# Batch 0 of a chunked attention with an MLP: transposes into one-bank PSUM tiles, values ahead of the last scores, zero matmuls moved, last copy on VectorE

## Chip, cores, metric

One core of a Trainium2 chip. The three later sets of runs were on three chips (8, 4 and 12 in the record: the runs a1 to a4, b1 to b4, c1 to c4), each with runs of the kernel before beside them. The metric is the device time of one execution in microseconds; the kernel before takes 233.71 us (median of the first three runs). PE is TensorE, ACT is ScalarE, DVE is VectorE, POOL is GpSimd.

Times of one kernel scatter here by about 2 us, more than the effect studied. So three things stand beside each time: the mean granted clock of the run (the share of TensorE's full clock that was let through), the start of the MLP in the trace, and the stretch from v2 to the MLP explained below.

## The reference, cut to what matters

```python
# q, k, v: (4 batches, 8 heads, 768, 64); 8 memory rows; windows of 32 queries
for c in range(768 // 32):
    k_full = concat([mem_k, k[:, :, c*32-16 : c*32+40]])     # v likewise
    scores = 0.125 * q_c @ k_full.T
    a = softmax(scores)
    out[:, :, c*32:c*32+32] = a @ v_full
x = out.transpose(0, 2, 1, 3).reshape(3072, 512)
h = x @ w_in                                                 # 512 -> 2048
s = sin(alpha * h)
y = (h + s * s / alpha) @ w_out                              # 2048 -> 512
```

## The kernel before, where it matters

The kernel works batch by batch. Batch 0's attention runs alone, ahead of batch 0's MLP, because nothing else has been loaded (in the first profile the loads of w_in are issued from 17.1 us on and land 6.5 to 12.9 us later). It is split into eight units, two for each pair of heads. A string gives the order in which their steps enter the engines' queues, each of which runs in order (in the first profile x2 starts at 20.69 us and v3, behind it in PE's queue, at 20.87): k and q are transposes of inputs, s scores, e exponentials, v values, x the transposes of a unit's result and their copy, and z a matmul on zeros. The tiles that this kernel's matmuls write are taken from two pools in PSUM: the smaller, [P, 512] in F32, are called one-bank tiles here, those of twice that size two-bank tiles.

```python
ORDER = (
    "k 0,q 0,memk 0,memv 0,k 1,s 0,e 0,z 1,s 1,e 1,q 1,k 2,s 2,e 2,s 3,v 0,q 2,e 3,k 3,x 0,v 1,q 3,s 4,e 4,x 1,"
    "s 5,e 5,v 2,z 1,s 6,e 6,x 2,v 3,z 1,s 7,e 7,x 3,z 1,v 4,z 1,v 5,x 4,z 1,v 6,x 5,z 1,v 7,x 6,z 1,x 7"
)
big = ...tile_pool(name="big", bufs=3, space=PSUM)   # tiles of two banks
smp = ...tile_pool(name="smp", bufs=2, space=PSUM)   # tiles of one bank

def spin(n, z=None):                       # z: n matmuls on zeros
    if z is None:
        z = smp.tile([P, 512], F32, name="z", tag="sm")
    for _ in range(n):
        nc.tensor.matmul(z[:], zeros[:, 0:P], zeros[:])

def pv(b, cells, pt):                      # v: values, then normalise on DVE
    ot = big.tile([P, 2, 512], F32, name="ot", tag="big")
    ...                                    # 8 matmuls into ot
    nc.vector.reciprocal(rv, otv[0:QW, :, :, D])
    nc.vector.tensor_tensor(out=x_blk..., in0=otv..., in1=rv..., op=ALU.mult)
    return x_blk, ot

def xt(dst, x_blk, ot, copy=nc.vector.tensor_copy):     # x: transpose, copy
    xtp = ot[:].bitcast(BF)[:, 0, 640:640 + KT * QW].rearrange("p (k c) -> p k c", k=KT)
    for kt in range(KT):
        nc.tensor.transpose(xtp[:, kt, :], x_blk[...], ident[0:QW, 0:QW])
    copy(dst, xtp)
...
# in the loop over ORDER
elif what == "e":
    ptl[n] = exps(cells[n], scl.pop(n))
    if n == 7:
        nc.scalar.activation(rows[:, 0:1], zeros[:, 0:1], ACTF.Sin)   # loads the sine table
elif what == "v":
    xbl[n] = pv(0, cells[n], ptl.pop(n))
elif what == "x":
    xt(xT[...], *xbl.pop(n), nc.vector.tensor_copy if n < 4 else nc.scalar.copy)
...
load_v(0, 0, 16)      # early; later, behind more of q and k:
load_v(0, 16, 32)     # values of units 2 and 3
load_v(0, 32, 64)     # values of units 4 to 7
```

The softmax here doesn't subtract the row's maximum and nothing guards it: scores larger than these inputs give would overflow.

## Time and profile before

| | kernel before, first profile |
|---|---|
| span in the trace | 232.2 us (the time adds about 1.8 us) |
| mean granted clock | 0.993 |
| first matmul of v2 | 19.27 us |
| first MLP matmul | 27.73 us |
| **v2 to MLP** | **8.46 us** |

"v2 to MLP" runs from the first value matmul of unit 2 to the first MLP matmul.

From the page of the kernel before, the slices of PE and of its clock (each digit is a tenth of a 5.8 us slice):

```profile
PE   7897899989999999999999999998999999899994
...
PEclk9998999999999999999999999999999999999999
```

PE is near full from slice 5 on, so an earlier MLP start should reach the end. The one dip of the clock, the 8 in the fourth slice, is half clock (0.50) over 3.4 us, from about 20.91 to 24.33 (read in windows of 0.1 us).

### The profile page before, as it was taken

What the parts mean: (1) busy time and instruction counts of PE and PEld (TensorE: products, weight loads), DVE (VectorE), ACT (ScalarE), POOL (GpSimd) and SP (SyncE); (2) the same over time, 40 slices, a digit from 0 to 9 for tenths busy, and PEclk for the clock granted to TensorE, in tenths of its full rate; (3) what the DMA queues carried; (4) which work ended last, traced back from release to release, by engine and by line L of the source; (5) the groups of instructions that cost most, each with busy time, mean ns of one, the idle gap of its engine ahead of it and who ended that gap; (6) DMA issues with size and microseconds to landing.
All of it is one profiled execution on the core that took longest, in us unless ns stands there. A gap on an engine that the chain in (4) does not pass through costs nothing.

```text
span 232.2 us, 4583 instructions
## 1 busy us (share of the span) xinstructions
PE 219.2 (94%) x1834; PEld 122.7 (53%) x1834; DVE 160.1 (69%) x287; ACT 153.0 (66%) x247; POOL 70.0 (30%) x80
## 2 busy tenths in 40 slices
PE   7897899989999999999999999998999999899994
PEld 3454565555446565654555656564555555453453
DVE  5775679888667897988467798887565458774110
ACT  3478689884887387898564877878664676880110
POOL 8999112595912115157300315020000020110000
PEclk9998999999999999999999999999999999999999
DMA  6999999999999910109992101010111010101112
GB/s 84 145 176 175 207 204 206 208 133 100 143 235 173 80 45 0 45 7 178 172 159 71 45 0 48 0 45 3 45 48 58 33 49 0 45 1 48 70 66 90
DMA packets 51805, 21.13 MB, mean 91 GB/s; under 512 B 36296, under 2 KB 48840, under 8 KB 51784
## 3 DMA queue, kind: packets, MB, share of 16 engines
q0 software_dynamic: 45568, 14.41, 68.7%
q1 hardware_dynamic: 6216, 6.43, 9.1%
q8 instruction: 14, 0.23, 0.4%
q14 instruction: 7, 0.06, 0.1%
HBM read 28.94 MB, written 6.29 MB: 152 GB/s over the span
## 4 chain that ended last, share of the span: by engine, by line
PE 64%; ACT 12%; DVE 11%; issue 5%; POOL 3%; DMA 2%; POOLq 1%; DVEq 0%; ACTq 0%
PE o L472 28%; PE hT L393 21%; DVE gT L422 5%; ACT u L405 4%; PE ot L301 3%; ACT pt L286 3%; PE sc L270 3%; DVE x_blk L306 2%; PE ot L316 2%; DMA k_bf<-in_k_dram 2%; DVE s L414 2%; ACT s L408 2%; PE tt_a L242 2%; PE o L461 2%; PE o L442 1%
## 5 line engine op out<-in xcount | busy, mean ns | idle before, releaser
L472 PE MATMUL o<-w_out_sb,gT 128*128 128x512 bf16 x336 | 90.0, 380 | 0.4 <-DVE gT L422 0.4
L393 PE MATMUL hT<-xT,w_in_sb 128*128 128x384 bf16 x488 | 87.1, 326 | 2.9 <-DVE gT L422 2.8
L422 DVE SCALAR_TENSOR_TENSOR gT<-s,inv_alpha,hT 128x768 bf16<-128x768 f32 x61 | 61.0, 1012 | 19.7 <-ACT s L408 11.6
L405 ACT ACTIVATE u<-hT,alpha_sb 128x768 f32<-128x768 f32 x61 | 54.7, 897 | 24.0 <-PE hT L393 22.9
L393 PEld LDWEIGHTS <-w_in_sb 128*128 128x128 bf16 x512 | 49.3, 98 | 37.5 <-issue 3.8
L286 ACT ACTIVATE pt<-sc,biasm 128x256 bf16<-128x256 f32 (+2 forms) x104 | 39.1, 470 | 15.1 <-PE sc L270 15.1
L472 PEld LDWEIGHTS <-gT 128*128 128x128 bf16 x336 | 29.3, 98 | 24.3 <-DVE gT L422 1.2
L410 POOL TENSOR_TENSOR s<-u 128x768 f32<-128x768 f32 x9 | 13.2, 1465 | 88.4 <-ACT u L405 61.3
L408 ACT ACTIVATE s<-u 128x768 f32<-128x768 f32 x32 | 27.0, 844 | 1.0
L414 DVE TENSOR_TENSOR s<-u 128x768 f32<-128x768 f32 x23 | 24.3, 1056 | 3.1 <-ACT u L405 3.0
L306 DVE TENSOR_TENSOR x_blk<-ot,rinv 96x512 bf16<-96x512 f32 x32 | 22.0, 687 | 1.1
L139 POOL DMA_DIRECT2D vw<-in_v_dram x24 | 22.0, 933 | 0.0
L216 POOL COPY pr<-q_bf 128x768 bf16<-128x768 bf16 x12 | 10.7, 894 | 35.4 <-PE tt_a L242 24.4
L430 DVE COPY o_sb<-o 128x512 f32<-128x512 f32 x12 | 8.3, 689 | 15.6 <-PE o L472 15.4
L430 ACT COPY o_sb<-o 128x512 f32<-128x512 f32 x11 | 6.4, 583 | 17.9 <-PE o L472 17.9
L305 DVE RECIPROCAL rinv<-ot 96x8 f32<-96x8 f32 x32 | 6.4, 201 | 15.8 <-PE ot L301 15.5
L301 PEld LDWEIGHTS <-pt 128*128 128x128 bf16 x256 | 12.4, 100 | 6.7 <-issue 2.2
L301 PE MATMUL ot<-vw,pt 128*128 128x65 bf16 x256 | 13.6, 197 | 0.9 <-ACT pt L286 0.9
L270 PEld LDWEIGHTS <-kTi 64*128 64x128 bf16 x256 | 6.9, 95 | 12.0 <-issue 5.9
L242 PEld LDWEIGHTS <-pr 128*128 128x128 bf16 x144 | 10.0, 98 | 5.9 <-DVE pr L216 0.9
L316 PE MATMUL ot<-ident,x_blk 96*128 96x96 bf16 x128 | 11.0, 208 | 2.1 <-DVE x_blk L306 2.0
L316 PEld LDWEIGHTS <-x_blk 96*128 96x128 bf16 x128 | 8.3, 98 | 8.4 <-DVE x_blk L306 3.8
(74 smaller groups left out, 171.1 us busy)
## 6 DMA issues: line engine op xcount, KB each, us to landing
out_dram<-o_sb SPq DMA_DIRECT2D x23, 256.0 KB, 2.0
k_bf<-in_k_dram POOLq DMA_DIRECT2D x3, 768.0 KB, 7.7
q_bf<-in_q_dram POOLq DMA_DIRECT2D x3, 768.0 KB, 12.4
vw<-in_v_dram POOLq DMA_DIRECT2D x6, 384.0 KB, 13.9
w_in_sb<-in_moe_w_in_dram POOLq DMA_DIRECT2D x4, 512.0 KB, 10.2
w_out_sb<-in_moe_w_out_dram POOLq DMA_DIRECT2D x2, 1024.0 KB, 24.8
k_bf<-in_k_dram POOLq DMA_DIRECT2D x4, 192.0 KB, 5.4
q_bf<-in_q_dram POOLq DMA_DIRECT2D x4, 192.0 KB, 5.4
```

The costliest lines, as they stand in the source:

```text
L139: nc.gpsimd.dma_start(dst, src)
L286: nc.scalar.activation(pt[:, 0:H * QW].rearrange("p (g e c) -> p e g c", g=4, e=2)[:, :, c0:c1, 32 * m:32 * m + 32], sc[:, :, 0:4 * QW].re ...
L301: nc.tensor.matmul(otv[:, n // 4, n % 4, :], pt[:, QW * n:QW * n + P], vws[b % 2][:, 2 * hp + n % 2, j, 0:D + 1])
L306: nc.vector.tensor_tensor(out=x_blk[:].rearrange("p (g e) d -> p g e d", g=2), in0=otv[0:QW, :, :, 0:D], in1=rv.unsqueeze(3).to_broadcast( ...
L316: nc.tensor.transpose(xtp[:, kt, :], x_blk[:, 2 * kt:2 * kt + 2, :].rearrange("p e d -> p (e d)"), ident[0:QW, 0:QW])
L393: nc.tensor.matmul(hts[hf][:, 0:HALF], w_in_sb[:, kt, P * ft:P * ft + P], xT[:, kt, HALF * hf:HALF * hf + HALF], start=(kt == 0), stop=(kt ...
L405: nc.scalar.activation(u[:], hT[:, :, 0:HALF], ACTF.Sin, scale=alpha_sb[:, ft:ft + 1])
L408: nc.scalar.activation(s2[:], u[:], ACTF.Square)
L414: nc.vector.tensor_tensor(out=s2[:], in0=u[:], in1=u[:], op=ALU.mult)
L422: nc.vector.scalar_tensor_tensor(out=gv, in0=s2[:], scalar=inv_alpha[:, ft:ft + 1], in1=hT[:, :, 0:HALF], op0=ALU.mult, op1=ALU.add)
L430: (nc.vector.tensor_copy if s % 2 == 0 else nc.scalar.copy)(o_sb[:], o[:])
L472: nc.tensor.matmul(o[:], gT[:, ft, P * s:P * s + P], w_out_sb[:, ft, :], start=(ft == 0), stop=(ft == FT - 1),)
```

## The change

The intent: PE should not stand behind a transpose that waits for DVE while a ready value product is queued behind it. So each v goes ahead of the previous x. To allow that, from unit 2 on x no longer uses v's tile, which is then free after the multiply. The values of unit 4 go ahead of the last scores. Zero matmuls move to where PE used to wait, with two ahead of each of the transposes. Copy 7 goes to DVE.

```diff
-    "s 5,e 5,v 2,z 1,s 6,e 6,x 2,v 3,z 1,s 7,e 7,x 3,z 1,v 4,z 1,v 5,x 4,z 1,v 6,x 5,z 1,v 7,x 6,z 1,x 7"
+    "s 5,e 5,z 1,v 2,s 6,e 6,z 2,v 3,x 2,v 4,s 7,e 7,x 3,v 5,x 4,v 6,x 5,v 7,x 6,x 7"
...
-        xtp = ot[:].bitcast(BF)[:, 0, 640:640 + KT * QW].rearrange("p (k c) -> p k c", k=KT)
+        if ot is None:
+            z = smp.tile([P, 512], F32, name="z", tag="sm")
+            spin(2, z)
+            xtp = z[:].bitcast(BF)[:, 0:KT * QW]
+        else:
+            xtp = ot[:].bitcast(BF)[:, 0, 640:640 + KT * QW]
+        xtp = xtp.rearrange("p (k c) -> p k c", k=KT)
...
-                xbl[n] = pv(0, cells[n], ptl.pop(n))
+                x_blk, ot = pv(0, cells[n], ptl.pop(n))
+                xbl[n] = x_blk, (ot if n < 2 else None)
...
-                   *xbl.pop(n), nc.vector.tensor_copy if n < 4 else nc.scalar.copy)
+                   *xbl.pop(n), nc.scalar.copy if n in (4, 5, 6) else nc.vector.tensor_copy)
```

## The prediction

> **What bounds the kernel now.** The part that changes is batch 0's attention: eight units (half a head pair each) go through s (scores, PE), e (exponentials, ACT), v (values into a PSUM tile `ot`, then reciprocal and multiply into `x_blk` on DVE), x (four PE transposes, then a copy into `xT`). z is a padding matmul on zeros. The MLP of batch 0 follows the last transpose in PE's order. I first read the page's slices: PE is 94% busy over the span, so a change here counts only by how much earlier the MLP starts. Then the chain of waits from 17 to 29 us (start, length, what):
>
> ```profile
> 17.96 1.26 ACT pt L286 x4
> ...
> 19.27 0.42 PE ot L301 x8
> ...
> 19.95 0.70 DVE x_blk L306
> 20.64 0.05 issue
> 20.69 0.34 PE ot L316 x4
> 21.04 0.45 PE ot L301 x8
> ...
> 24.14 0.70 DVE x_blk L306
> 24.84 0.05 issue
> 24.88 0.34 PE ot L316 x4
> 25.23 0.22 PE z L162
> 25.44 0.26 PE ot L301 x8
> ...
> 26.80 0.70 DVE x_blk L306
> 27.50 0.05 issue
> 27.55 0.34 PE ot L316 x4
> 27.89 1.14 PE hT L393 x7
> ```
>
> L301 is v, L306 the multiply, L316 the transposes, L393 the MLP. In front of x2 (20.69) and x4 (24.88) the next v stands behind a transpose that waits for DVE's multiply: v3 has its data, but starts only when x2 is through. So each unit pays v, reciprocal, multiply and transpose in series. The MLP's first matmul is at 27.73 in the timeline (the chain puts its boundary at 27.89). PE's order holds it behind x7, though its first six matmuls need only units 0 to 5.
>
> Next the busy times and granted clock in consecutive 3.42 us stretches, cut where the clock changes (columns: stretch, length, busy of PE, PEld, DVE, ACT, POOL, then clock, DMA share, GB/s):
>
> ```profile
> 14.12:17.54 3.42, 3.24 (x61) 2.05 (x59) 2.59 (x11) 3.15 (x9) 3.42 (x5) 1.00 2.11 158
> 17.54:20.96 3.42, 1.89 (x42) 1.27 (x37) 1.87 (x4) 3.42 (x12) 3.42 (x5) 0.99 2.11 159
> 20.96:24.38 3.42, 3.26 (x39) 2.03 (x37) 2.05 (x6) 2.73 (x8) 2.75 (x4) 0.51 1.23 203
> 24.38:27.80 3.42, 2.65 (x43) 1.73 (x41) 3.18 (x9) 2.29 (x5) 0.00 (x0) 1.00 1.25 206
> ```
>
> PE was 55% busy (1.89 of 3.42) in the second stretch and had half the clock in the third. With 77% (2.65) it kept its clock. Last, ACT's timeline:
>
> ```profile
> 22.38 1.35 ACT L286 ACTIVATE pt<-sc,biasm 128x256 bf16<-128x256 f32 x4 [0.67 <-PE sc L270]
> 23.75 1.28 ACT L369 ACT_TABLE_LOAD   x1
> 25.04 0.20 ACT L369 ACTIVATE rows<-zeros 128x1 f32<-128x1 bf16 x1
> 25.26 0.48 ACT L319 COPY xT<-ot 128x384 bf16<-128x384 bf16 x1
> ```
>
> ACT idles 0.67 us before the last exponentials, since s7 stands behind x2, v3 and a z at half clock (s7 starts at 21.83; e6 ends at 21.70). Then the table load bars ACT until 25.24, and the x copies 4 to 7 come after it.
>
> [...] Here 0.43 to 0.57 us recur on PE before x1, v2 and x2; only that before v2 is of this kind (it waits for e4, which frees the tile it takes, while its own exponentials were done long before).
>
> **The change, part by part.** (1) From unit 2 on, transposes no longer land in `ot` but in a fresh one-bank tile, of which there are two. So `ot`, one of three two-bank tiles shared with the scores, is free after the multiply, not after the copy. (2) Each such x has two zero matmuls in front: 12 new ones. The z in the order go from seven to three from s5 on, so there are 8 more, each 0.215 us of PE issue time at full clock (two take 0.43). Most lie in waits. (3) v3 goes in front of x2, v4 in front of s7, and every later v in front of the previous x, so PE no longer waits for a multiply with a ready v behind it. (4) Copy 7 moves from ACT (0.48) to DVE (0.34 to 0.36); in the old order it was not on the path, since the first ACT work of the MLP begins at 29.23, after copy 7 ended at 28.41.
>
> I lay the new order out with durations from this trace: v issues in 0.26 (ends after 0.41), transposes 0.17 (0.34), s 0.26, reciprocal 0.20, multiply 0.69, hand-overs 0.02 to 0.05, all at full clock. Until 18.76 nothing changes.
> - z, then v2 at 19.27 as before (waits for e4, 19.22); multiply 2 ends 20.64.
> - s6 19.53, two z to 20.22, v3 at 20.53 (its tile comes from e5, about 20.48), against 20.87 to 21.04; multiply 3 from 21.20 to 21.89.
> - x2's zeros 20.79, transposes 21.22; its copy on DVE follows multiply 3, to 22.25. v4 at 21.39, multiply 4 from 22.40 to 23.09 (before: from 24.14).
> - s7 at 21.76, e7 from 22.12 to 23.47 (before: 23.73), table load and dummy until 24.98.
> - x3, v5 at 22.62, multiply 5 to 24.27; x4's transposes end at 23.65, but its copy waits for ACT: 25.00 to 25.48. v6 23.48, multiply 6 to 25.11; x5's transposes end 24.66, its copy 25.88; v7 24.49, multiply 7 to 25.97.
> - x6 needs the one-bank tile of x4, free at 25.48: zeros 25.52 to 25.95, transposes to 26.12. x7: zeros to 26.55 (tile of x5 free at 25.88), transposes to 26.72. MLP from 26.74.
>
> So 27.73 minus 26.74 is 1.0 us. The path that ends last turns from DVE's multiplies into e7, table load, copy of x4, the tile for x6, and four zero matmuls (0.86 us, which are pure cost there). Copies 6 (ACT, to 26.80) and 7 (DVE, to 27.26) are in time for the seventh and eighth MLP matmuls at about 27.7 and 27.9.
>
> **Does the clock hold?** In 17.54 to 20.96 the gap before v2 shrinks from 0.43 to about 0.14 and that before x2 (0.53) to 0.14; 0.57 before x1 stays. Idle 0.85 of 3.42, 75% busy, against 55% that lost the clock and 77% that kept it. I give it 0.7.
>
> **Rivals.** First: the clock falls anyway (0.3). Then x2's zeros, x3's and v4, v5 run at half speed from 20.96; the same laying out gives s7 at 22.17, e7 to 24.05, ACT free at 25.56, copy 4 to 26.06, x6 to 26.70, multiply 7 to 27.02, MLP at 27.3. Gain 0.4 us. Second: the zeros and the two one-bank tiles cost what the order wins; the MLP then starts at 27.7 and the time stays 233.7. For it speaks that 1.3 us of ACT table load now stand in front of copy 4 with x6 behind it; against it, that copy 4 begins at 25.26 even before. Third: a fixed transfer swallows the gain. The second half of w_out lands latest, 26.9 us after its issue at 23.2, so 50.1; it is wanted only after the first eight tiles of two output blocks started at 50.1, some 3.5 us later. Input weights of the fourth quarter land by 19.4 + 12.9 = 32.3 and are wanted past 40. Both leave room for 1 us, and the batch 1 loads are issued by POOL behind MLP work and shift with it. So an earlier start should reach the end whole.
>
> **Range and chances.** 0.7 x 1.0 + 0.3 x 0.4 = 0.8 us: 233.71 - 0.8 = 232.9. Before's runs lie 233.12 to 233.95, so about 0.4 either way from noise alone; both branches with it give 232.2 to 233.7. Two per cent is 4.7 us, more than five times anything I can construct: within 2% is 0.97, faster 0.02, slower 0.01.
>
> **What would show it right or wrong.** Right: the first MLP matmul near 26.7; granted clock 1.00 through 21 to 24; no idle on ACT over 0.5 us before e7; multiply 4 before 23.2; x6's zeros waiting for ACT's copy of x4; the whole difference already there at the MLP's start. Half clock in 21 to 24 with the MLP at 27.3 would be the first rival. An MLP start 1 us earlier with the same end would be the third. Wrong altogether: v3 or s7 waiting for a PSUM tile longer than laid out, since which of the three tiles they take is inferred from one wait.

One passage, before "Here 0.43 to 0.57 us recur", is cut from the prediction, since it told of the hardware what no trace of this case shows (the two measured figures in it stand in the views above it: the clock of 0.51 from 20.96 to 24.38, and 1.28 us for the table load); "of this kind", just behind the cut, means a wait for a PSUM tile. That the busy share of PE in one stretch tells the clock after it was my estimate, from the stretches shown (55% busy, then a clock of 0.51; 77% busy, and the clock kept at 1.00).

## The result, and the profile after

The time did not move: 233.78 us median (233.47 to 233.90, 4 runs) against 233.76 (233.12 to 233.95, 4 runs). The ratio is 1.0004, with a 95% interval of 0.9982 to 1.0025. A ratio here is the mean time of one kernel's fast runs over that of the other's of the same rounds, so it is not quite the ratio of the medians. The record lists every run of this study as fast, those with a clock dip too.

The prediction of 232.9 was 0.9 us too low and its range missed the result by 0.08 us. Yet the trace of the changed kernel ends 0.5 us earlier than that of the kernel before, 231.7 against 232.2. Both have to be explained.

First the changed kernel's consecutive stretches, cut as in the prediction (busy of PE first, the clock third from the right):

```profile
17.54:20.96 3.42, 2.74 (x41) 1.63 (x42) 1.87 (x5) 3.42 (x12) 3.34 (x5) 1.00 2.40 147
20.96:24.38 3.42, 2.85 (x51) 2.03 (x49) 2.87 (x8) 2.30 (x7) 2.83 (x4) 1.00 1.24 207
```

PE is 80% busy (2.74 of 3.42) where it was 55%, and the clock stays at 1.00 in the next stretch. This step went as foreseen. Next the changed kernel's chain of waits over the same part (start, length, what; its line numbers are 6 or 7 higher from the transposes on, so L322 is x and L400 the MLP):

```profile
16.60 5.22 DMA vw<-in_v_dram
21.82 0.14 issue
21.96 0.40 PE ot L301 x8
22.36 0.29 PE sc L270 x8
22.65 0.02 issue
22.68 1.35 ACT pt L286 x4
24.03 0.02 issue
24.05 1.28 ACT L375
...
25.55 0.38 ACT xT L325
25.92 0.04 issue
25.96 0.59 PE z L162 x2
26.56 0.17 PE z L322 x4
26.73 0.43 PE z L162 x2
27.16 0.17 PE z L322 x4
27.33 3.90 PE hT L400 x24
```

From the last exponentials on this is the path that was laid out: table load, copy 4 (the line at 25.55), zeros of unit 6, zeros of unit 7, MLP. The head of it is new. The chain begins at a transfer of v that lands at 21.82, and v4 (21.96) waits for it. PE's timeline shows the wait:

```profile
21.96 0.40 PE L301 MATMUL ot<-vw,pt 128*128 128x65 bf16 x8 [0.57 <-DMA vw<-in_v_dram]
```

The last scores stand behind v4, and all else behind them. ACT's timeline shows what this costs, between e6, which ended at 21.58, and e7:

```profile
22.68 1.35 ACT L286 ACTIVATE pt<-sc,biasm 128x256 bf16<-128x256 f32 x4 [1.10 <-PE sc L270]
```

ACT idles 1.10 us there, where it idled 0.67 us before (and only 0.16 us in the profiles of the old order at full clock, b1 and b2 below). The MLP starts at 27.17. From v2 (19.14) that is 8.03 us, not the 7.47 that were laid out (26.74 - 19.27).

### The profile page after: what moved, and what is told of

It reads as the page before. It is cut to its first block, busy times and chain, and to the rows that moved or that the text cites. A ratio compares the mean times of both kernels' runs of the same rounds, so it can differ in the third digit from the quotient of the medians.

```text
span 231.7 us, 4595 instructions
## 1 busy us (share of the span) xinstructions
PE 219.4 (95%) x1842; PEld 122.7 (53%) x1842; DVE 160.1 (69%) x288; ACT 152.4 (66%) x246; POOL 69.9 (30%) x80
## 4 chain that ended last, share of the span: by engine, by line
PE 62%; ACT 12%; DVE 9%; issue 5%; DMA 5%; POOL 4%; POOLq 1%; DVEq 0%; ACTq 0%
PE o L479 28%; PE hT L400 21%; DVE gT L429 5%; ACT u L412 4%; PE ot L301 3%; DMA q_bf<-in_q_dram 3%; ACT pt L286 3%; PE sc L270 2%; DMA vw<-in_v_dram 2%; DVE s L421 2%; ACT s L415 2%; PE tt_a L242 2%; PE ot L322 2%; PE o L468 2%; PE o L449 1%
## 5 line engine op out<-in xcount | busy, mean ns | idle before, releaser
L400 PE MATMUL hT<-xT,w_in_sb 128*128 128x384 bf16 x488 | 87.1, 326 | 2.9 <-DVE gT L429 2.8
L400 PEld LDWEIGHTS <-w_in_sb 128*128 128x128 bf16 x512 | 49.3, 98 | 37.5 <-issue 3.8
L301 PEld LDWEIGHTS <-pt 128*128 128x128 bf16 x256 | 11.7, 98 | 7.0 <-issue 2.7
L162 PE MATMUL z<-zeros 128*128 128x512 bf16 x40 | 12.8, 426 | 1.9 <-DVE zeros L155 1.2
L301 PE MATMUL ot<-vw,pt 128*128 128x65 bf16 x256 | 13.0, 193 | 1.1 <-DMA vw<-in_v_dram 0.6
L322 PEld LDWEIGHTS <-x_blk 96*128 96x128 bf16 x128 | 8.7, 97 | 7.5 <-DVE x_blk L306 1.7
```

Source lines behind the costliest of these rows:

```text
L301: nc.tensor.matmul(otv[:, n // 4, n % 4, :], pt[:, QW * n:QW * n + P], vws[b % 2][:, 2 * hp + n % 2, j, 0:D + 1])
L400: nc.tensor.matmul(hts[hf][:, 0:HALF], w_in_sb[:, kt, P * ft:P * ft + P], xT[:, kt, HALF * hf:HALF * hf + HALF], start=(kt == 0), stop=(kt ...
```

## The experiments

All numbers of the twelve runs. "Wait for v" is PE's wait for v from memory ahead of v4.

| kernel | v2 | MLP | v2 to MLP | wait for v | mean time (runs) | lowest clock |
|---|---|---|---|---|---|---|
| before, first profile (half clock) | 19.27 | 27.73 | 8.46 | none | | |
| b1_before (full clock in its profile) | 20.66 | 28.37 | 7.71 | none | 234.12 (6) | 0.983 |
| after, first profile | 19.14 | 27.17 | 8.03 | 0.57 | 233.74 (4) | 0.999 |
| a1_after | 20.30 | 28.21 | 7.91 | 0.45 | 233.97 (6) | 0.998 |
| a2_scores_first | 19.73 | 26.79 | 7.06 | none | 233.27 (6) | 0.998 |
| a3_no_tail_zeros | 20.60 | 27.31 | 6.71 | none | 233.11 (6) | 0.998 |
| a4_copy4_dve | 19.20 | 27.67 | 8.47 | 1.43 | 233.76 (6) | 0.998 |
| b2_before_clock_held | 19.38 | 27.10 | 7.72 | none | 233.40 (6) | 1.000 |
| b3_scores_first_no_tail | 19.95 | 27.10 | 7.15 | 0.24 | 233.29 (6) | 0.991 |
| b4_no_value_wait (wrong result) | 19.63 | 27.00 | 7.37 | none | 233.42 (6) | 0.999 |
| c1_no_new_zeros | 19.17 | 26.01 | 6.84 | 0.16 | 235.57 (6) | 0.977 |
| c2_tiles_alone | 20.37 | 28.08 | 7.71 | none | 234.81 (6) | 0.985 |
| c3_copy7_act | 18.95 | 27.46 | 8.51 | 1.04 | 233.90 (4) | 0.999 |
| c4_zeros_in_waits | 19.43 | 26.63 | 7.20 | 0.31 | 233.15 (6) | 0.998 |

In the profiles of both unedited kernels and of seven of the ten edits, span minus MLP start is 204.5 us within 0.1. So what happens up to the MLP start goes into the time whole. The exceptions are c1 (206.0), c2 and c3 (both 204.8).

### a1_after: the changed kernel again

No edit.

> The changed kernel again, unedited, for more rounds and the clock and span of each run. In the one profile of each kernel that is at hand the first MLP matmul starts at 27.17 us against 27.73 and the span is 231.7 against 232.2, yet the timed medians are equal (233.78, 233.76). Theory A (the 0.56 us are real, the early medians of four runs too coarse): ratio to the kernel before 0.9975 to 0.9985. Theory B (the kernel before loses its clock at 21 us only in some runs, its profiled one among them, and the others are as fast as the changed one): ratio 0.999 to 1.001, and a profile with the MLP start again near 27.2.

Ratio 0.9998 (0.9971 to 1.0025). This lies in the range of theory B, but the interval takes in that of theory A too, so the ratio alone does not decide; b1_before will. Of the eleven runs of the kernel before on the same chip in this set, three had a mean clock of 0.993 or less; these took 234.24 to 234.97 us. The six runs of the changed kernel had 0.998 or more. The MLP start was not near 27.2 but at 28.21, since the loads came later (PE waited 0.76 us for k at 16.43): v2 itself had moved from 19.14 to 20.30.

### a2_scores_first: only v4 and the last scores swapped back

```diff
-...v 3,x 2,v 4,s 7,e 7,x 3,v 5,...
+...v 3,x 2,s 7,e 7,v 4,x 3,v 5,...
```

> Only the order of v4 and s7/e7 is swapped back (last scores in front of the values of unit 4). Theory (v4 waits until about 21.8 us for the last quarter of v from memory, and the last scores, exponentials, table load and copy of unit 4 stand behind it): e7 starts at about 21.6 to 22.0 instead of 22.68, ACT waits under 0.4 us before it instead of 1.10, the copy of unit 4 starts near 24.5 to 24.9 instead of 25.45, the MLP at 26.2 to 26.6 instead of 27.17, the time 0.6 to 1.0 us under the changed kernel (ratio to it 0.996 to 0.9975). Rival (the last scores wait for the exponentials of unit 6 or for their PSUM tile, so the order does not matter): e7 still at 22.4 or later, MLP start within 0.2 us of 27.17.

ACT's timeline in a2_scores_first:

```profile
18.32 5.33 ACT L286 ACTIVATE pt<-sc,biasm 128x64 bf16<-128x64 f32 x16
23.67 1.28 ACT L375 ACT_TABLE_LOAD   x1
```

All sixteen exponentials of units 4 to 7 now run without a gap, and the table load follows at once. v2 to MLP falls from 7.9 to 8.0 down to 7.06 us. The mean time is 0.70 us under a1_after of the same rounds (233.27 against 233.97); the ratio to the kernel before is 0.9973 (0.9949 to 0.9996). The MLP start, foreseen for 26.2 to 26.6, was 26.79; v2 had come 0.59 us later than in the profile that the estimate used. The theory holds: the placement of v4 ahead of the last scores is what costs.

### a3_no_tail_zeros: no zeros ahead of the transposes of units 6 and 7

```diff
-            spin(2, z)
+            spin(nz, z)          # nz = 0 for units 6 and 7, else 2
```

> The four zero matmuls ahead of the transposes of units 6 and 7 are left out. Theory (they are pure cost at the end of the path, 0.86 us of PE issue, of which the wait for the tile of unit 5 takes some back): transposes of unit 6 at about 25.96, of unit 7 at 26.3, MLP at 26.5 instead of 27.17, 0.65 us less. Rival (they fill waits that stay): MLP start unchanged within 0.15 us.

v2 to MLP is 6.71 us, the shortest. That is 1.2 to 1.3 us less than the changed kernel, but not all of it belongs to the zeros: in this profile the loads held v2 back until 20.60, and v4 then found its values there. Counted from v4, it is 4.63 us (22.68 to 27.31) against 5.21 in both profiles of the changed kernel (21.96 to 27.17, 23.00 to 28.21). So 0.58 us are gained. Counted from the end of PE's wait for copy 4, where the zeros lie, it is 0.55 us (26.76 to 27.31) against 1.21 in both profiles (25.96 to 27.17, 27.00 to 28.21). So the zeros cost 0.66 us, as the 0.65 expected; the other 0.08 us lie between v4 and the last scores, also in b4 below, where v4 doesn't wait either. Mean time 233.11, ratio 0.9966 (0.9939 to 0.9993).

### a4_copy4_dve: copy 4 on DVE

```diff
-                   *xbl.pop(n), nc.scalar.copy if n in (4, 5, 6) else nc.vector.tensor_copy)
+                   *xbl.pop(n), nc.scalar.copy if n in (5, 6) else nc.vector.tensor_copy)
```

> The x copy of unit 4 goes to DVE instead of ACT, so that the one-bank tile that unit 6 takes does not wait for the table load. Theory (0.68 us wait of PE for this copy sets the end): the zeros of unit 6 start near 25.1 instead of 25.96; DVE's later multiplies shift by about 0.3; MLP near 26.8 instead of 27.17, 0.35 us less. Rival (DVE's last multiply, pushed back by the copy, takes over wholly): MLP at 27.1 or later.

From v4 to the MLP it takes 4.79 us (22.88 to 27.67), 0.42 less than the changed kernel and close to the 0.35 expected. The zeros of unit 6 no longer wait for the table load (26.04, straight behind v7). Yet the time is 233.76, ratio 0.9994 (0.9970 to 1.0017). In this profile v landed late and v4 waited longer than in any other, as its PE timeline shows:

```profile
22.88 0.40 PE L301 MATMUL ot<-vw,pt 128*128 128x65 bf16 x8 [1.43 <-DMA vw<-in_v_dram]
```

By its number, 27.67, the MLP start falls to the rival ("27.1 or later"), but through the wait for v and not through DVE. The saving behind v4 is real in the trace, but whether it reaches the time is not shown.

### b1_before: the kernel before, a second profile

No edit.

> The kernel before, unedited, for a second profile. Since the loads shift all of this stretch by up to 1 us from run to run, the measure is the time from the first matmul of v2 to the first MLP matmul: 8.46 us in its first profile, 8.03 and 7.91 in two profiles of the changed kernel. Of eleven runs of the kernel before, three had a mean clock of 0.993 or less and were the slow ones (234.2 to 235.0). Theory (half clock after 21 us is an accident of some runs, and without it the old order is as fast as the new one or faster): a profile at full clock gives 7.5 to 7.8 us; again half clock gives 8.4 to 8.5. Rival (the old order is slower whatever the clock): 8.2 or more at full clock.

The profile fell in a full-clock run. Its PE timeline at v2 and at the MLP's start:

```profile
20.66 0.40 PE L301 MATMUL ot<-vw,pt 128*128 128x65 bf16 x8 [0.44 <-ACT pt L286]
...
28.37 0.82 PE L393 MATMUL hT<-xT,w_in_sb 128*128 128x384 bf16 x4
```

At full clock the old order takes 7.71 us, less than the 7.91 and 8.03 of the changed kernel, in which v4 waited. The theory holds. Ratio to the runs of the same kernel beside it: 0.9989 (0.9956 to 1.0021), which shows how coarse such a comparison is.

Over the three sets the kernel before ran 39 times with its clock listed, these six included. In 13 runs it was 0.993 or less, and these have a mean of 234.68 us. The other 26 have a mean of 233.76. The ten runs of the changed kernel all had 0.998 or more, with a mean of 233.88. It is thus 0.8 us faster than the kernel before with a dip and 0.1 us slower, within noise, than that kernel without it.

The size of the dip orders the runs further: six of the 13 had 0.992 or 0.993, like the first profile, with a mean of 234.30 us, and seven had 0.983 to 0.985, with a mean of 235.00. By estimate the latter lost about twice as much clock as the first profile (0.015 against 0.007); where they lost it is not traced. The dips also came unevenly, in 3 of 11 runs of the first set, 9 of 17 of the second and 1 of 11 of the third. The changed kernel has no run in the second set, but the six of b4 below, with the same instructions in the same order, are from it and had 0.999 or more.

### b2_before_clock_held: the kernel before with three more zeros in waits

```diff
-    "s 5,e 5,v 2,z 1,s 6,e 6,x 2,v 3,...
+    "s 5,e 5,z 1,v 2,z 1,s 6,e 6,z 2,x 2,v 3,...
```

> The kernel before with three more zero matmuls in waits of PE (one ahead of v2, two ahead of x2), nothing else. Theory (they hold the clock and lie in waits): every run's clock 0.998 or more, v2 to MLP 7.5 to 7.8 us, mean time 0.1 to 0.3 us under the kernel before, the slowest runs gone. Rival (zeros do not decide the clock): some runs at 0.993 or less as before.

All six runs had clock 1.000 and took 233.12 to 233.91 us, while seven of the eleven runs beside them of the kernel before had 0.993 or less. Ratio 0.9958 (0.9931 to 0.9984). v2 to MLP is 7.72, as in b1 at full clock, so the three zeros cost nothing. The stretch after s5 in this kernel:

```profile
17.54:20.96 3.42, 2.42 (x43) 1.36 (x41) 1.94 (x5) 3.42 (x12) 2.69 (x5) 1.00 2.25 147
```

PE is 71% busy there (2.42 of 3.42) against 55%. In this set, holding the clock alone gains 0.99 us on average (234.39 to 233.40), without the new order. That is more than the 0.1 to 0.3 expected because the kernel before dipped in seven of eleven runs; against the other four, with a mean of 233.79, it is 0.4 us.

### b3_scores_first_no_tail: both repairs

The edits of a2 and a3 together.

> Changed kernel with both repairs: last scores ahead of v4, no zeros ahead of the transposes of units 6 and 7. Theory (both costs are on one path and the rest of it is DVE's chain of multiplies): v2 to MLP about 6.7 to 6.9 us against 7.06 with the first repair alone, time 0.9 to 1.2 us under the changed kernel and the kernel before, ratio 0.995 to 0.9965. Rival (the two gains overlap wholly): as the first repair alone, ratio 0.997 to 0.998.

Ratio 0.9952 (0.9920 to 0.9985), the lowest of all, but against rounds in which the kernel before dipped often; the mean of 233.29 is that of a2. v2 to MLP is 7.15, no shorter than a2's. From v4 it is 4.37 us against a2's 4.57, so leaving out the zeros of units 6 and 7 gives only 0.2 us here. Transposes 6 and 7 then waited 0.25 and 0.49 us for DVE's multiplies, so DVE's chain sets the end. The expected 6.7 to 6.9 was too low, since v4 still waits for v (0.24 us). One run of six had clock 0.991 and took 234.23. The ratio falls in the theory's range, but only through the dips beside it; by v2 to MLP the rival is nearer.

### b4_no_value_wait: unit 4 reads values that are there

```diff
-                x_blk, ot = pv(0, cells[n], ptl.pop(n))
+                x_blk, ot = pv(0, cells[2 if n == 4 else n], ptl.pop(n))
```

> Wrong on purpose: the changed kernel, but unit 4 reads the values of unit 2, which are there long before; all instructions and their order stay. Theory (the wait for v from memory delays v4 and through it the last scores, the table load and copy 4): no wait of PE for v ahead of v4, e7 starts within 0.6 us of the end of e6, v2 to MLP 7.4 to 7.6 us instead of 8.0, time 0.4 to 0.6 us under the changed kernel. Rival (another wait takes its place, such as the PSUM tile of the last scores): v2 to MLP still 7.9 or more.

ACT's timeline in b4_no_value_wait:

```profile
22.51 1.35 ACT L286 ACTIVATE pt<-sc,biasm 128x256 bf16<-128x256 f32 x4 [0.43 <-PE sc L270]
```

Same instructions, same order, but the wait ahead of e7 falls from 1.10 to 0.43 us and v2 to MLP to 7.37, close to the 7.47 laid out in the prediction. v4 starts 2.09 us after v2 (21.72 - 19.63); the prediction had 2.12. The mean of 233.42 is 0.55 us under that of a1_after, though from another set of runs. The ratio, 0.9959 (0.9932 to 0.9985), is again against rounds with many dips. The step missing from the path was the arrival of v; what else was off on it comes to 0.1 us.

### c1_no_new_zeros: the new order without zeros

```diff
-    "s 5,e 5,z 1,v 2,s 6,e 6,z 2,v 3,x 2,...
+    "s 5,e 5,v 2,s 6,e 6,v 3,x 2,...
-            spin(2, z)
```

> The changed order and the one-bank tiles, but no zero matmul from s5 on. It asks what the zeros are for. Theory (they hold the clock, and the four ahead of units 6 and 7 cost 0.65 us): some of the six runs have a mean clock of 0.993 or less, as 12 of 28 of the kernel before had and 0 of 10 of the changed one; v2 to MLP about 7.3 to 7.4 us where the profile has full clock (changed kernel 7.9 to 8.0), about 8 with half clock; mean time between 233.2 and 234.0. Rival (the new order keeps PE busy enough by itself): all six runs at 0.998 or more, mean about 233.2.

Slower by 0.7% (ratio 1.0073, 1.0037 to 1.0108), outside the expected range (mean 235.57). All six runs had 0.993 or less, five of them 0.977 or 0.978. The profiled run was the mildest of the six (233.84, clock 0.993). In it v2 to MLP is 6.84 us, less than the 7.3 to 7.4 expected, and the MLP starts earliest of all, at 26.01, but then runs at half clock (columns as above, a stretch of 3.40 us, then of 1 us):

```profile
22.30:25.70 3.40, 1.73 (x36) 1.31 (x32) 3.25 (x8) 3.33 (x9) 1.49 (x2) 1.00 1.23 198
...
24.00:25.00 1.00, 0.59 (x12) 0.56 (x13) 0.93 (x4) 0.99 (x3) 0.00 (x0) 1.00 1.26 204
25.00:26.00 1.00, 0.62 (x8) 0.48 (x8) 0.65 (x1) 0.96 (x3) 0.00 (x0) 0.84 1.23 205
26.00:27.00 1.00, 1.00 (x7) 0.49 (x5) 0.60 (x3) 0.17 (x1) 0.00 (x0) 0.50 1.25 209
```

From 22.30 to 25.70 PE was busy 1.73 of 3.40 us, 51%, and the first 24 MLP matmuls then took 5.58 us against 4.07. So the zeros of the change are what keeps it from being a loss. Where the other five runs lost their clock is not traced.

### c2_tiles_alone: one-bank tiles in the old order

Old order, old zeros, copies 4 to 7 on ACT; only the tile of x changes, without `spin(2, z)`.

> The kernel before with its own order and zeros; only the transposes from unit 2 on go to one-bank tiles without zeros. Theory (the PSUM tile is not what the old order waits for, DVE's multiplies are): v2 to MLP 7.6 to 7.8 us at full clock, 8.4 to 8.5 with half clock, some runs at 0.993 or less, ratio to the kernel before 0.998 to 1.002. Rival (tiles freed at the multiply speed the old order up): v2 to MLP under 7.4 at full clock.

v2 to MLP is 7.71 us, as in the kernel before at full clock: in the old order the tile is not what is waited for. The time, however, is worse: 234.81 on average, ratio 1.0040 (1.0015 to 1.0065), with 234.50 to 234.66 even in the three runs at 0.999 or 1.000. In the trace 0.3 us of it lie behind the MLP's start (204.8 instead of 204.5), as a wait of ACT ahead of the sine of one MLP tile:

```profile
37.74 0.90 ACT L411 ACTIVATE u<-hT,alpha_sb 128x768 f32<-128x768 f32 x1 [0.33 <-PE hT L399]
```

The kernel before has no gap there. PE is named, but its matmuls of that tile had ended at about 37.35, so another wait must be behind it. I did not find which (the chain of waits calls it "issue"), and the rest of the 0.4% stays open too.

### c3_copy7_act: copy 7 back on ACT

```diff
-                   *xbl.pop(n), nc.scalar.copy if n in (4, 5, 6) else nc.vector.tensor_copy)
+                   *xbl.pop(n), nc.scalar.copy if n in (4, 5, 6, 7) else nc.vector.tensor_copy)
```

> The changed kernel with copy 7 back on ACT. Theory (not on the path): v2 to MLP 7.9 to 8.1 us as in the changed kernel, the same ratio within noise, no wait of PE for this copy in the first MLP matmuls. Rival: a wait of the eighth MLP matmul for copy 7, over 0.2 us.

Ratio 0.9999 (0.9964 to 1.0033). v2 to MLP is 8.51, over the 7.9 to 8.1 expected, with a wait of 1.04 us for v; from v4 it is 5.21 us (22.25 to 27.46), that of the changed kernel. No MLP matmul waits for copy 7. The same 0.33 us wait of ACT as in c2 appears in the MLP (at 37.12), and 204.8 us follow the MLP start. So copy 7 is off the path up to the MLP, as predicted. With the one-bank tiles, copy 7 on ACT (c2, c3) comes with a 0.3 us wait later that the prediction did not see; in the kernel before, with copy 7 on ACT too but the old tile, it is absent. Its cause is open, each of c2 and c3 has one profile, and the four runs do not show it in the time.

### c4_zeros_in_waits: a version for use

a2's order, and one zero matmul ahead of the transposes of units 6 and 7.

> Last scores ahead of v4, and one zero matmul instead of two (or none) ahead of the transposes of units 6 and 7, which waited 0.25 and 0.49 us without any. Theory (zeros that lie in waits cost nothing and hold the clock, which fell in one of six runs without them): all clocks 0.998 or more, v2 to MLP 7.0 to 7.2 us, mean time 233.0 to 233.3, ratio to the kernel before 0.994 to 0.997. Rival (they still push the end): v2 to MLP 7.3 or more.

233.15 us on average, all clocks 0.998 or more, ratio 0.9969 (0.9942 to 0.9996), v2 to MLP 7.20, at the edge of what was expected. Its result is correct, and it is faster than the kernel before by 0.3%, though the interval ends at 0.9996. One of its runs took 234.18 at clock 1.000; that this was late loads is likely but not traced. Among a2, a3, b2, b3 and c4 the runs don't decide.

## Why the prediction was wrong, point by point

Two steps of the prediction failed. Of its 0.99 us, 0.75 (8.46 - 7.71) was a dip of the clock in the profiled run of the kernel before, which most of its runs don't have. The other 0.24 (7.71 - 7.47) asked for v4 at 21.39, without a wait for v from memory; with that wait, v2 to MLP was 8.03 us. Of the signs that it named, full clock from 21 to 24, the wait of x6 for copy 4 and the whole difference at the MLP's start came true; the MLP near 26.7 (27.17) and less than 0.5 us of idle on ACT (1.10) did not. The wait of v3 or s7 for a PSUM tile that it feared did not appear: PE's timeline shows no idle time before them (20.38 and 22.29).

**The clock.** The step that the new order and its zeros hold the clock was right (80% busy for an estimated 75%; 0 of 10 runs dipped). What failed is the other side of the difference. I took "27.73 minus 26.74" as the gain over 233.71 us, but 27.73 belongs to a run at half clock, which took 234.0 us. 233.71 is the median of three others, of 233.12 to 233.95 us. Their clocks are not on record, but all are shorter than every run of this kernel on record at 0.993 or less (the profiled one is the shortest). That the profiled run was longer than all three could have been seen beforehand. At full clock the old order would have reached the MLP 7.71 us after v2 (b1, b2: 7.71 and 7.72). Even against the path exactly as laid out, 7.47 us, that leaves 0.24 us and not 1.0. I gave the changed kernel a chance of dipping and the kernel before none of not dipping. A third of its runs dip (13 of 39), so by keeping the clock the change removes 0.92 / 3 = 0.3 us on average over these sets (0.92 is 234.68 - 233.76).

**The arrival of v.** The step "v4 at 21.39" asked only for PE, the PSUM tile and the exponentials. It did not ask when the second half of v is there (a2's expectation calls it the last quarter). v4 started at 21.96 behind a transfer that landed at 21.82. In six profiles v4 stands in that place with its own values: in after, a1, a4 and c3 it waited 0.45 to 1.43 us, in c1 0.16, and in a3, where v2 came late, not at all. In the first profile of the kernel before, v4 comes 3.94 us after v2 (23.21 - 19.27), later than the longest wait for v let it start anywhere (3.68 in a4), so that trace shows no wait for v. The rival "a fixed transfer swallows the gain" was named, but only the weights were checked. b4 removes the wait alone and gets 7.37 us.

**What the wait takes along.** Because the last scores stand behind v4, e7 began at 22.68 instead of 22.12, and the table load, copy 4, the zeros of unit 6 and the MLP moved with it. a2 takes the last scores out of that queue and gains 0.7 us. The 0.67 us of idle on ACT that the new order was to shorten were themselves mostly an effect of the half clock (0.16 at full clock in b1 and b2).

**The tail.** "x6 needs the one-bank tile of x4" was right: PE waited 0.68 us for copy 4. "Four zero matmuls, pure cost" was right in kind, with 0.66 us measured (a3) of 0.86 us of issue time (25.96 to 26.39 and 26.56 to 27.00 in the changed kernel), and 0.2 us once the scores are first (b3). From v4 to the MLP the prediction had 5.35 us (26.74 - 21.39); measured 5.21.

**The second rival.** "The zeros and the two one-bank tiles cost what the order wins" came true in the time, but not in its sign, an MLP start at 27.7 (27.17). Its reason was incomplete: the wait for v adds to the zeros.

**The sum.** Against the 26 full-clock runs of the kernel before, the change loses 0.1 us (233.88 - 233.76); against the 13 others it wins 0.8 (234.68 - 233.88). Two to one, as in these sets, that is (13 x 0.80 - 26 x 0.12) / 39 = 0.2 us, which runs that scatter by 0.3 to 0.5 us (standard deviation) don't show. The range was too narrow because both branches started from one profile.

**The end.** That an earlier MLP start reaches the end whole was right: 204.5 us follow it in both kernels. The prediction's "some 3.5 us" of room for w_out was in fact 5.7 us (the 17th of these matmuls starts at 55.83), which doesn't change the reading.

## What to carry to other kernels

Before a difference to a profile is called a gain, ask whether the profiled run was like the median one: here the profiled run was longer than the three timed ones, and the mean clock of each run showed that a third of them dip. When an instruction is moved forward, ask again for every operand when it is there, above all for data from memory whose landing the old place hid, and keep whatever feeds a long chain (here the last scores, ahead of a table load) out of the queue behind it. Zero matmuls that keep the clock cost nothing here where they lay in waits (b2: clock 1.000 in all six runs, 7.72 us against 7.71), and most of their issue time where there was no wait (a3: 0.66 of 0.86 us).

## What else the traces show

- Half clock followed stretches of 3.4 us in which PE was 55% (first profile of the kernel before) and 51% busy (c1_no_new_zeros), and the stretch at 77% in the first profile was followed by full clock. No share at which the clock falls is settled here: a4_copy4_dve had 57% busy (1.94 of 3.42 us, from 20.96) and kept its clock (1.00 in that stretch and the next). One kernel dips in the middle in some runs and not in others, 13 of 39 at a mean cost of 0.9 us. Why it dips in just those runs is not shown.
- The table load took 1.28 us, and nothing besides it shows in the changed kernel's first profile: e7 ends at 24.03, the load starts at 24.05 and the next ACT instruction at 25.34.
- In the same profile loads of v, of 15 to 192 KB, took 5.2 to 6.8 us from issue to landing (median of the two of 192 KB 6.5), beside other loads. v2, which comes after such loads, started between 18.95 and 20.66 us in different profiles. This scatter from run to run is larger than the effect of the change.
